# VectorE's maxima, reciprocals and scalings as jobs of their own, and Strassen's scheme in the first channel product from batch 5 on

## The chip, the cores and the metric

The kernel runs on one core of one Trainium2 chip. The metric is the time of one execution on the device, in microseconds (us); smaller is better. TensorE is called PE here (PEld is its weight load), VectorE DVE, ScalarE ACT, GpSimd POOL, and SyncE SP, as the profile calls them.

## What is computed

Two blocks in a row, on 8 batches of 576 rows. The first is linear attention with 8 heads of 64 columns and 128 random features, the second an MLP mixer over rows ("tokens") and columns ("channels"). Cut to what matters:

```python
def phi(x):                                   # x: q or k, scaled by 64 ** -0.25
    h = einsum('bhsd,md->bhsm', x, omega) - sum(x * x) / 2
    return exp(h - max(h)) / sqrt(m)
kv  = einsum('bhsm,bhsd->bhmd', phi(k), v);  z = sum(phi(k), over s)
x   = einsum('bhsm,bhmd->bhsd', phi(q), kv) / (einsum('bhsm,bhm->bhs', phi(q), z) + 1e-6)

h   = maximum(x.T @ w_tok1, 0) @ w_tok2       # over the 576 rows, 256 wide inside
u   = x + h.T
out = u + maximum(u @ w_ch1, 0) @ w_ch2       # 512 columns, 1536 wide inside
```

## The kernel before

Everything runs in fp16 with sums in fp32. Each batch has 512 main rows and 64 tail rows; the tail rows of all batches are gathered and go through the channel block together at the end, as a ninth "batch" (c == B in the code).

A batch passes through these stages. **Loads**: POOL's DMAs write q and k to scratch in DRAM as fp16, SP's transposing DMAs bring them back with heads along partitions (`load_transposed`), into rings `kT` and `qT` of three buffers; `v` has a ring of three too. **Attention** (`attention`): PE makes the features of k (`kp`) and q (`qp`) for a pair of heads, 64-row matmuls that run two side by side; ACT takes the exponential out of PSUM. DVE takes the largest feature of each row of `kp` (`reduce_max`, into `km`) and its reciprocal, which goes into the last column of `vs`; POOL scales `v` by it. PE makes `kv`, then for each head the numerators and the denominator (function `num`, five matmuls of 65 columns into one PSUM bank), and DVE takes the reciprocal of the denominators (`rc`) and multiplies (`num_out`), which gives `x`. **Token mixing** (`token_mix`): two products on PE, a ReLU between them, and DVE's additions that give `u`; one transposing DMA on SP makes `uT` of it. `token_tail` does the tail rows of a pair of batches. **Channel mixing** (`channel_mix`): the first product, u @ w_ch1, its ReLU into `r3`, and the second product.

Strassen's scheme does a product of 2 x 2 blocks with seven block products in place of eight, for extra sums. The second channel product uses it from batch 1 on (`channel_out_fast`). The first uses it for batches `c >= FAST1` (`channel_in_fast`), with `FAST1 = 6`; before that it is the plain product of line 1120, 48 matmuls of 512 columns whose 12 banks ACT (in some cases DVE) reads with a ReLU. In the fast form each of three passes makes seven products of four matmuls of 256 columns in three PSUM banks X, Y, Z; ACT or DVE copies X out between products (`kept`, `go_a`), DVE adds the copies (`summed`, line 1066), and some ReLUs are done in place afterwards. Four sums of `u` blocks (`go_u`) go ahead of it on DVE, and once in the kernel four sums of weight blocks (`first_weights`). The summed weights and the sums of u live in buffers taken from the rings: `HOME` and `OF_V` name one buffer each of kT, qT and v, and the copies take one of x and one of r1. From `FAST1` on each of these five rings has a buffer less.

No scheduler decides the order. The code lists jobs (`plan.add`, 1293 of them), each for one engine, with what it depends on. The table `ORDER` gives the order in which their instructions are written out, `SLOT` the buffer of a ring or the PSUM bank that each takes, and `MOVED` the engine of some jobs. Each engine then runs its own instructions strictly in that order. A job's function may issue several instructions, and nothing of the same engine comes between them.

Of the kernel before, what the change touches and what calls it, by code (L numbers as in the profile page):

```python
# [9 lines left out]
FP32 = mybir.dt.float32  # L10
# [57 lines left out]
]  # L68
SLOT = (
# [22 lines left out]
class Job:  # L92
    def __init__(self, eng, cost, key, fn, deps, take, give, rows, wire):
        self.eng, self.cost, self.key, self.fn = eng, cost, key, fn
        self.deps, self.take, self.give = deps, take, give
        self.rows, self.wire = rows, wire
        self.end = None
        self.heavy = False

FAST1 = 6


def covered(name):

    kind = name[0][0] if isinstance(name[0], tuple) else name[0]
    if kind in ("X", "Y", "Z"):
# [71 lines left out]
def kernel(  # L180
# [92 lines left out]
    t_kmt = ring(2, [P, 4], FP16, "kmt")  # L273
    kt_nb = sb([P, 2, 2], FP32, "kt_nb")
    t_rct = ring(2, [P, 4], FP16, "rct")
    t_rc = ring(4, [P, 2, NJ + 1], FP32, "rc")


    nat = {}
# [946 lines left out]
```

## Time and profile before

| | |
|---|---|
| time, median of 3 runs | 279.74 us (279.21 to 279.97) |
| the profiled execution, its own time | 279.72 us |
| its span, first to last instruction | 277.9 us |
| busy share of the span | PE 96%, DVE 84%, ACT 56%, POOL 33% |
| granted clock of PE, mean | 0.974 |
| DVE instructions | 487 |
| DMA | 39.69 MB, 143 GB/s on average |

The 1.8 us between the span and the execution's own time lie around the first and the last instruction. A busy PE includes the latency of each matmul, which overlaps the next one, so PE's real load is read from the distance between starts. A group's row gives the busy time, the mean duration of one instruction in ns, and the idle time of the engine just ahead of them.

### The profile page before, as it was taken

The page shows a single profiled execution, that of the slowest core. Times are in us where ns is not written, and L with a number is a line of the kernel's source. Part 1 is how long each engine was busy: PE and PEld are TensorE (multiplying, and loading weights), DVE is VectorE, ACT ScalarE, POOL GpSimd, SP SyncE. Part 2 cuts the span into 40 slices and gives each one's busy share as a digit, 9 for nine tenths or more (in the row PEclk, how much of TensorE's full clock was granted, in tenths as well). Part 3 has the DMA queues.
Part 4 walks back from the last instruction along what each step waited for, and adds up shares of the span by engine and source line. Part 5 has one row for each costly group of instructions (what it writes and reads, how often), then busy time and mean ns, then how long its engine had stood idle before and what let it go on. Part 6 is the DMA issues. An engine that isn't in the chain of part 4 may idle for free.

```text
span 277.9 us, 6547 instructions
## 1 busy us (share of the span) xinstructions
PE 265.6 (96%) x2624; PEld 179.5 (65%) x2624; DVE 233.7 (84%) x487; ACT 154.5 (56%) x318; POOL 91.6 (33%) x115
## 2 busy tenths in 40 slices
PE   5789999999999999999999999999999999999993
PEld 2657546443657755665677646764597688888882
DVE  1698828499999889996998799999997999889992
ACT  2797994049667427644567544878835425153410
POOL 8597794007510773048006910333400000000000
PEclk9559999999999999999999999999999999999999
DMA  7999999999997999995989993970060062030125
GB/s 160 200 205 169 182 185 204 164 151 211 182 226 164 164 211 162 170 196 89 189 181 211 203 195 85 167 179 4 18 174 0 2 150 97 0 153 0 65 105 136
DMA packets 80622, 39.69 MB, mean 143 GB/s; under 512 B 63984, under 2 KB 76144, under 8 KB 80400
## 3 DMA queue, kind: packets, MB, share of 16 engines
q0 software_dynamic: 31696, 17.61, 44.0%
q1 hardware_dynamic: 47696, 18.52, 30.5%
q10 hardware_dynamic: 1200, 3.15, 3.2%
q8 instruction: 20, 0.33, 0.5%
q14 instruction: 10, 0.08, 0.1%
HBM read 35.95 MB, written 16.52 MB: 189 GB/s over the span
## 4 chain that ended last, share of the span: by engine, by line
PE 88%; DVE 4%; DMA 3%; ACT 2%; issue 1%; ACTq 0%; DVEq 0%
PE bank L965 25%; PE bank L1120 22%; PE bank L1053 9%; PE bank L833 5%; PE bank L820 5%; PE bank L1155 4%; PE bank L711 3%; PE bank L699 3%; DMA wc<-in_k_dram 3%; PE bank L777 3%; PE bank L744 2%; DVE o L954 1%; PE bank L887 1%; DVE x L787 1%; PE bank L859 1%; ACT qp L557 1%
## 5 line engine op out<-in xcount | busy, mean ns | idle before, releaser
L301 ACT ACTIVATE r<-bank 128x512 f16<-128x512 f32 (+1 forms) x82 | 46.3, 604 | 43.5 <-PE bank L1120 25.6
L1120 PE MATMUL bank<-uT,wc 128*128 128x512 f16 x280 | 67.9, 379 | 0.0
L306 POOL TENSOR_TENSOR vs<-v,vs 128x512 f16<-128x512 f16 x32 | 34.3, 1072 | 79.5 <-DVE vs L725 49.8
L1120 PEld LDWEIGHTS <-wc 128*128 128x128 f16 x280 | 24.8, 98 | 25.7 <-issue 2.6
L965 PEld LDWEIGHTS <-r 128*128 128x128 f16 x384 | 36.7, 98 | 6.9 <-issue 1.3
L557 ACT ACTIVATE qp<-bank 128x512 f16<-128x512 f32 x64 | 36.6, 624 | 8.0 <-PE bank L711 5.2
L557 ACT ACTIVATE kp<-bank 128x512 f16<-128x512 f32 x64 | 36.5, 617 | 7.2 <-PE bank L699 7.0
L723 DVE TENSOR_REDUCE km<-kp 128x8 f16<-128x1024 f16 x32 | 38.5, 1205 | 0.6 <-ACT kp L557 0.4
L787 DVE TENSOR_TENSOR x<-bank,rc 128x320 f16<-128x320 f32 x62 | 30.5, 492 | 2.1
L965 PEld LDWEIGHTS <-S 128*128 128x128 f16 x288 | 28.2, 98 | 5.3 <-issue 0.6
L999 POOL DMA_DIRECT2D out_dram<-o x1 | 0.7, 665 | 73.4 <-issue 73.4
L965 PE MATMUL bank<-T,r 128*128 128x256 f16 x192 | 23.8, 273 | 0.0
L965 PE MATMUL bank<-wc,r 128*128 128x256 f16 x192 | 23.6, 273 | 0.0
L965 PE MATMUL bank<-T,S 128*128 128x256 f16 x192 | 23.6, 273 | 0.0
L303 DVE TENSOR_SCALAR r<-bank 128x512 f16<-128x512 f32 (+1 forms) x26 | 17.1, 663 | 7.5 <-PE bank L820 4.9
L954 DVE TENSOR_TENSOR o<-u,bank 128x512 f32<-128x512 f16 x28 | 19.0, 679 | 2.8 <-PE bank L965 2.6
L836 DVE TENSOR_TENSOR u<-x,bank 128x512 f16<-128x512 f16 x28 | 17.6, 680 | 0.5 <-ACT r L297 0.5
L777 PEld LDWEIGHTS <-qp 128*128 128x128 f16 x256 | 13.7, 100 | 6.2 <-issue 0.2
L954 DVE TENSOR_TENSOR o<-o,bank 128x512 f32<-128x512 f32 (+1 forms) x25 | 15.1, 612 | 2.7 <-PE bank L965 2.5
L1053 PEld LDWEIGHTS <-wc 128*128 128x128 f16 x144 | 13.8, 98 | 2.6 <-issue 0.6
L777 PE MATMUL bank<-kvsb,qp 128*128 128x65 f16 x256 | 15.0, 196 | 0.0
L711 PE MATMUL bank<-qT,omT 64*128 64x512 f16 x64 | 12.5, 410 | 1.7 <-ACT qT L297 1.7
(151 smaller groups left out, 470.5 us busy)
## 6 DMA issues: line engine op xcount, KB each, us to landing
out_dram<-o SPq DMA_DIRECT2D x10, 512.0 KB, 2.9
q<-in_q_dram POOLq DMA_DIRECT2D x6, 576.0 KB, 9.6
wc<-in_moe_w_ch_dram POOLq DMA_DIRECT2D x4, 768.0 KB, 10.8
k<-in_k_dram POOLq DMA_DIRECT2D x6, 512.0 KB, 7.8
v<-in_v_dram POOLq DMA_DIRECT2D x6, 512.0 KB, 10.0
out_dram<-o ACTq DMA_DIRECT2D x4, 512.0 KB, 2.7
r<-in_q_dram POOLq DMA_DIRECT2D x4, 288.0 KB, 7.1
v<-in_v_dram POOLq DMA_DIRECT2D x4, 256.0 KB, 9.5
```

The costliest lines, as they stand in the source:

```text
L301: nc.scalar.activation(out=out, in_=in_, func=AF.Relu)
L306: (nc.gpsimd if eng == "POOL" else nc.vector).tensor_tensor(**kw)
L557: nc.scalar.activation(out=out, in_=in_, func=AF.Exp, bias=0.0, scale=1.0)
L711: nc.tensor.matmul(ps[e], omT[half[e]], t[half[e], 2 * hp : 2 * hp + 2, 0:R], start=True, stop=True)
L723: nc.vector.reduce_max(out=mx, in_=kpv, axis=AX.X)
L777: nc.tensor.matmul(ps[:, k, j * 65 : (j + 1) * 65], st, s[:, i, 0 : D + 1], start=True, stop=True)
L787: nc.vector.tensor_tensor(out=t_x[place("x", b)][:, :, (2 * hp + hs[0]) * D : (2 * hp + hs[0] + n) * D].rearrange("p j (i d) -> p i j d", ...
L836: nc.vector.tensor_tensor(out=t_u[place("u", b)][:, j, :], in0=t_x[place("x", b)][:, j, :], in1=bank(n), op=ALU.add)
L954: nc.vector.tensor_tensor(out=o, in0=a, in1=ps, op=ALU.add)
L965: nc.tensor.matmul(ps[:, j * DH : (j + 1) * DH], a[:, cb, j * P : (j + 1) * P], w[:, cb, :], start=(bank_of(b, j0) not in held and j == j0 ...
L1053: nc.tensor.matmul(ps[:, 2 * P * t : 2 * P * t + 2 * P], a_[:, k, cb * P : (cb + 1) * P], m[:, :, k, :], start=(begin and t == 0 and k == ...
L1120: nc.tensor.matmul(ps, wc1[:, db, cb * P : (cb + 1) * P], moving(db), start=(db == 0), stop=(db == ND - 1))
```

## The change

Seven edits of structure, and new tables:

- The job that took the maximum of `kp` and its reciprocal becomes two jobs, with a ring `km` of four buffers for the maxima (two before, used in turn).
- The same for the tail rows of k: maximum, reciprocal and product with the mask become three jobs.
- The reciprocal and the scaling of a head's numerators become two jobs, with a ring `rc` of six buffers.
- The two additions of `token_tail` become two jobs, each of which gives its batch's `x` free.
- `FAST1` goes from 6 to 5: batch 5's first channel product takes the fast form too, and the ring buffers for it are taken a batch earlier.
- `ORDER`, `SLOT` and `MOVED` are written anew, for 1431 jobs. No other constant changes.

```diff
@@ ORDER, its second row: the same jobs, with later numbers
-49, 18, 46, 69, 71, 45, 77, 120, 51, 90, 50, 105, 122, 82, 52, 106, 17, 107, 19, 53, 121, 54, 83, 111, 92, 123, 91, 30, 108, 124, 126, 72, 112, 79,
+49, 18, 46, 69, 71, 45, 77, 127, 51, 93, 50, 110, 129, 82, 52, 111, 17, 112, 19, 83, 128, 53, 54, 84, 116, 95, 130, 94, 30, 113, 117, 131, 133, 72,
...
-FAST1 = 6
+FAST1 = 5
...
-             "kvsb": 3, "ktt": 2, "x": 3, "r1": 3, "u": 3, "uT": 3, "r3": 2, "S": 1, "V": 1, "s": 3, "o": 2, "bank": 8}
+             "kvsb": 3, "ktt": 2, "x": 3, "r1": 3, "u": 3, "uT": 3, "r3": 2, "S": 1, "V": 1, "s": 3, "o": 2, "km": 4, "rc": 6, "bank": 8}
...
-    t_km = ring(2, [P, 8], FP16, "km")
+    t_km = ring(COUNT["km"], [P, 8], FP16, "km")
...
-    t_rc = ring(4, [P, 2, NJ + 1], FP32, "rc")
+    t_rc = ring(COUNT["rc"], [P, NJ + 1], FP32, "rc")
...
-            j_ktm = add("DVE", 1.2, kkt + 0.01, kt_max, deps=[*j_kte, j_msk], take=[("vbd", b)] if dma_in else [])
+            j_ktm = add("DVE", 0.7, kkt + 0.01, kt_red, deps=[*j_kte, *kt_parts.get(b - 2, [])])
...
+            j_ktr = add("DVE", 0.2, kkt + 0.01, kt_rec, deps=[j_ktm])
...
+            j_ktm = add("DVE", 0.2, kkt + 0.01, kt_vb, deps=[j_ktr, j_msk], take=[("vbd", b)] if dma_in else [])
+            kt_parts[b] = [j_ktr, j_ktm]
...
             def km(hp=hp):
                 kpv = t_kp[place("kp", (b, hp))].rearrange("p c e m -> p (c e) m")
-                mx, vs = t_km[hp % 2], t_vs[place("vs", (b, hp))]
-                nc.vector.reduce_max(out=mx, in_=kpv, axis=AX.X)
+                nc.vector.reduce_max(out=t_km[place("km", (b, hp))], in_=kpv, axis=AX.X)
+            j_m = add("DVE", 1.2, at_["km"], km, deps=je, take=[("km", (b, hp))])
+            def km_rec(hp=hp):
                 with nc.allow_low_precision(reason="fp16 operand of the matmul"):
-                    nc.vector.reciprocal(out=vs[:, :, D], in_=mx)
-            j_m = add("DVE", 1.4, at_["km"], km, deps=je, take=[("vs", (b, hp))])
+                    nc.vector.reciprocal(out=t_vs[place("vs", (b, hp))][:, :, D], in_=t_km[place("km", (b, hp))])
+            j_m = add("DVE", 0.2, at_["km"], km_rec, deps=[j_m], take=[("vs", (b, hp))], give=[("km", (b, hp))])
...
+                def rec(where=where, rc_of=rc_of):
+                    nc.vector.reciprocal(out=rc_of(), in_=where()[:, 0, 0 : 5 * 65].rearrange("p (j d) -> p j d", d=65)[:, :, D])
+                kno = HEAD["no"][2 * hp + hs[0]] if b == 0 else at_["no"]
+                j_r = add("DVE", 0.22, kno - 0.3, rec, deps=[j_n], take=[n_rc])
...
-                    last_x.append(add("DVE", 0.1 + 0.52 * len(hs), kno, num_out, deps=[j_n], take=[("x", b)], give=[at]))
+                    last_x.append(add("DVE", 0.62, kno, num_out, deps=[j_r], take=[("x", b)], give=[at, n_rc]))
...
-        def uadd():
-            for o in range(2):
-                s = half[o]
+        j2 = []
+        for o in range(2):
+            def uadd(o=o, s=half[o]):
                 nc.vector.tensor_tensor(out=t_ut[s, pair_], in0=t_x[place("x", 2 * pair_ + o)][s, NJ, :], in1=bank(n)[s], op=ALU.add)
-        j2 = add("DVE", 1.36, key, uadd, deps=[j1], give=[("bank", n), ("x", 2 * pair_), ("x", 2 * pair_ + 1)])
+            j2.append(add("DVE", 0.69, key, uadd, deps=[j1], give=[("bank", n), ("x", 2 * pair_ + o)]))
```

The new tables show in the order of each engine's instructions. On PE it is the same up to the middle of batch 3's channel products, the 1006th matmul, and another after it.

The first place is DVE in batch 4's attention, where it scales the heads into the `x` buffer 119 (`rc` are the reciprocals, `bank` the PSUM banks with the numerators). Before:

```order
L786 RECIPROCAL rc_144<-bank_67 128x5
L787 TENSOR_TENSOR x_119<-bank_67,rc_144 128x5x64
L786 RECIPROCAL rc_143<-bank_63 128x5
L787 TENSOR_TENSOR x_119<-bank_63,rc_143 128x5x64
L786 RECIPROCAL rc_143<-bank_65 128x5
L787 TENSOR_TENSOR x_119<-bank_65,rc_143 128x5x64
```

The same place in the changed program, where lines 798 and 802 are the reciprocal and the scaling:

```order
L798 RECIPROCAL rc_144<-bank_65 128x5
L798 RECIPROCAL rc_148<-bank_70 128x5
L802 TENSOR_TENSOR x_119<-bank_70,rc_148 128x5x64
L798 RECIPROCAL rc_147<-bank_67 128x5
L798 RECIPROCAL rc_145<-bank_68 128x5
L802 TENSOR_TENSOR x_119<-bank_67,rc_147 128x5x64
L802 TENSOR_TENSOR x_119<-bank_65,rc_144 128x5x64
L802 TENSOR_TENSOR x_119<-bank_64,rc_143 128x5x64
```

A scaling no longer has to follow its own reciprocal; most now read one that was made two or more instructions earlier.

The second place is DVE where the last weight sum (`wc<-wc`) and the sums of u stand for the first batch that takes the fast form. Before, that is batch 6 (`uT_127`), amid batch 7's attention:

```order
L306 TENSOR_TENSOR wc_80<-wc_80 128x2x768
L306 TENSOR_TENSOR S<-r_131 128x768
L306 TENSOR_TENSOR r_131<-r_131 128x3x256 x2
L306 TENSOR_TENSOR S<-S,r_131 128x768 x2
L954 TENSOR_TENSOR o_133<-u_125,bank_66 128x2x256
L786 RECIPROCAL rc_144<-bank_68 128x5
L787 TENSOR_TENSOR x_119<-bank_68,rc_144 128x5x64
L954 TENSOR_TENSOR o_132<-o_132,bank_70 128x2x256
L786 RECIPROCAL rc_144<-bank_69 128x5
L787 TENSOR_TENSOR x_119<-bank_69,rc_144 128x5x64
L306 TENSOR_TENSOR kT_89<-uT_127 128x512
```

In the changed program it is batch 5 (`uT_129`), amid batch 6's attention, which begins to write `x_119` only after both additions of the tail rows (`ut`):

```order
L904 TENSOR_TENSOR ut<-x_119,bank_70 64x512
L904 TENSOR_TENSOR ut<-x_120,bank_70 64x512
L312 TENSOR_TENSOR wc_80<-wc_80 128x2x768
L965 TENSOR_TENSOR o_132<-o_132,bank_65 128x2x256
L312 TENSOR_TENSOR kT_88<-uT_129 128x512
L312 TENSOR_TENSOR qT_85<-uT_129,kT_88 128x512
L965 TENSOR_TENSOR o_133<-u_124,bank_63 128x2x256
L303 CAST kvsb_117<-bank_67 128x2x65
L312 TENSOR_TENSOR uT_129<-uT_129 128x2x256
L312 TENSOR_TENSOR v_92<-uT_129,qT_85 128x512
L798 RECIPROCAL rc_146<-bank_69 128x5
L802 TENSOR_TENSOR x_119<-bank_69,rc_146 128x5x64
```

The preparation has moved a batch earlier, and the buffers that it uses are now kT_88 and qT_85, not kT_89 and qT_86.

The third place is SP's queue around batch 7's transposing loads. Before:

```order
L841 DMA_TRANSPOSE uT_129<-u_125 128x16x128
L391 DMA_TRANSPOSE kT_88<-k_7_158 128x1x2304
L1006 DMA out_dram<-o_133 128x1024
L898 DMA_TRANSPOSE uTt<-ut 128x4x128
L391 DMA_TRANSPOSE qT_85<-q_7_157 128x1x2304
L841 DMA_TRANSPOSE uT_127<-u_126 128x16x128
```

In the changed program (line 397 is the load, 852 the transpose of u, 909 that of the tail rows, 1017 a store):

```order
L852 DMA_TRANSPOSE uT_129<-u_125 128x16x128
L397 DMA_TRANSPOSE kT_89<-k_7_162 128x1x2304
L909 DMA_TRANSPOSE uTt<-ut 128x4x128
L397 DMA_TRANSPOSE qT_86<-q_7_161 128x1x2304
L1017 DMA out_dram<-o_132 128x1024
L852 DMA_TRANSPOSE uT_127<-u_126 128x16x128
```

Batch 7's k and q go into the buffers of batch 5 (89 and 86), where they went into those of batch 4 before; a store now stands between them and the transpose of batch 6's u.

More of the change, by code (lines that the diff above doesn't have):

```diff
@@ L23 @@
 3, 0, 4, -1, 14, 7, 5, 2, -2, 6, 10, 1, -3, -4, 9, -5, 8, -6, -7, 12, -8, 11, 13, 41, 21, 38, 42, 47, 22, 39, 43, 40, 48, 67, 76, 68, 44, 78, 16, 70,
[44 rows of a table removed]
[50 rows of a table added]
 ]
 SLOT = (
-    "00010203010320452601510723430621530411262070250331643571201036502170160175130200671135462167340123201201243172160135071304056117337611405242"
-    "13273212406745307413212050264111070260542300073561240011137632413005114726002203221170220145370200325123340671206511070032241107321540103201"
-    "03221711413101305210117250024012410731211721602132040570040260230570105337110602202613531013270127021523120021003514126240340212031451203032"
-    "41501013607204010631112714023363060140123010700341200603001222417502456140325317630401502630207412036051222306433131263411051015001251652212"
-    "17420335106022716422067513013651427021650113122704252064750022201364170051213500121641000756420657142526126202141024061102150670314510226130"
-    "7150014306102710200210171032071505"
+    "00010203010320452601510723430620153041112620702502331643357120103650201170213601754130502067113541260167342103201002124317016013507112043256"
+    "11733711640035413223730462501750432752130563212000415161270410052300273011450021611713451320032657211022406324147303245250672013023063044536"
+    "35217120104172006325142763105042322106324711501134026002211147302035022413512376011104024526132071054200103760124002413532002715430073006511"
+    "01225316124030412023107151034520743222354154042740201503671410140761153203301600256113211110026523710201230135205167323114001010723430602554"
+    "11670121327324115002534406501273200310650742013356022223124037051143202615170161422302034612146312500046100343313114015210056231102643100605"
+    "23071431112020302542170003514113203043120720370722250504712073310250170251136050214103105002671421060040126205700265110002410063507106"
@@ L76 @@
 )
 MOVED = {
-43: "ACT", 51: "ACT", 54: "ACT", 60: "ACT", 63: "ACT", 65: "ACT", 75: "DVE", 85: "ACT", 129: "ACT", 139: "DVE", 141: "DVE", 145: "ACT", 147: "DVE",
-163: "ACT", 169: "DVE", 171: "ACT", 175: "DVE", 179: "ACT", 190: "ACT", 194: "ACT", 228: "ACT", 242: "DVE", 256: "DVE", 265: "DVE", 278: "DVE", 280:
-"DVE", 286: "DVE", 300: "DVE", 324: "ACT", 399: "DVE", 426: "DVE", 428: "DVE", 432: "DVE", 434: "DVE", 484: "DVE", 498: "DVE", 552: "DVE", 556: "DVE",
-562: "DVE", 593: "ACT", 594: "ACT", 634: "DVE", 662: "DVE", 690: "DVE", 692: "DVE", 700: "DVE", 702: "DVE", 768: "DVE", 796: "DVE", 864: "ACT", 972:
@@ L82 @@
-"DVE", 988: "DVE", 1003: "ACT", 1105: "DVE", 1125: "DVE", 1127: "DVE", 1134: "DVE", 1157: "DVE", 1165: "ACT", 1203: "DVE", 1233: "DVE", 1242: "ACT",
-1244: "ACT", 1282: "SP", 1283: "SP", 1285: "ACT", 1286: "SP", 1287: "ACT", 1288: "SP", 1289: "ACT", 1290: "SP", 1291: "ACT", 1292: "SP",
+43: "ACT", 51: "ACT", 54: "ACT", 60: "ACT", 63: "ACT", 65: "ACT", 75: "DVE", 86: "ACT", 137: "ACT", 149: "DVE", 151: "DVE", 155: "ACT", 157: "DVE",
+173: "ACT", 179: "DVE", 181: "ACT", 185: "DVE", 189: "ACT", 200: "ACT", 204: "ACT", 244: "ACT", 261: "DVE", 278: "DVE", 289: "DVE", 303: "DVE", 305:
@@ new lines @@
+"DVE", 311: "DVE", 325: "DVE", 349: "ACT", 438: "DVE", 457: "DVE", 465: "DVE", 473: "DVE", 497: "ACT", 543: "DVE", 588: "DVE", 610: "DVE", 614: "DVE",
+728: "DVE", 760: "DVE", 772: "DVE", 796: "ACT", 825: "DVE", 876: "DVE", 935: "DVE", 950: "ACT", 951: "ACT", 952: "ACT", 977: "ACT", 1023: "DVE", 1040:
+"DVE", 1057: "DVE", 1086: "DVE", 1114: "DVE", 1125: "ACT", 1126: "ACT", 1197: "DVE", 1267: "DVE", 1279: "DVE", 1286: "DVE", 1288: "DVE", 1293: "DVE",
+1302: "ACT", 1379: "ACT", 1382: "ACT", 1419: "ACT", 1421: "SP", 1427: "ACT", 1428: "SP",
@@ L562, in vbd_of @@
         return first_vbd[:, b] if b < NPE else t_vbd[place("vbd", b)]
+    kt_parts = {}
     def attention(b, key, step):
@@ L629, in attention, with kt_red, kt_rec, kt_vb @@
                 j_kte.append(add("ACT", 0.3, kkt, kt_exp, deps=[j_kt], take=[("kpt", b)], give=[("bank", (n_kt, e))]))
-            def kt_max():
-                kp = t_kpt[place("kpt", b)].rearrange("p g e m -> p (g e) m")
-                mx, rc, vb = t_kmt[b % 2], t_rct[b % 2], vbd_of(b)
-                nc.vector.reduce_max(out=mx, in_=kp, axis=AX.X)
+            def kt_red():
+                nc.vector.reduce_max(out=t_kmt[b % 2], in_=t_kpt[place("kpt", b)].rearrange("p g e m -> p (g e) m"), axis=AX.X)
+            j_ktm = add("DVE", 0.7, kkt + 0.01, kt_red, deps=[*j_kte, *kt_parts.get(b - 2, [])])
+            def kt_rec():
                 with nc.allow_low_precision(reason="fp16 operand of the matmul"):
-                    nc.vector.reciprocal(out=rc, in_=mx)
+                    nc.vector.reciprocal(out=t_rct[b % 2], in_=t_kmt[b % 2])
+            j_ktr = add("DVE", 0.2, kkt + 0.01, kt_rec, deps=[j_ktm])
+            def kt_vb():
                 nc.vector.tensor_tensor(
-                    out=vb[:, :, 0:nh, D],
-                    in0=rc.unsqueeze(2).broadcast_to((P, 4, nh)),
+                    out=vbd_of(b)[:, :, 0:nh, D],
+                    in0=t_rct[b % 2].unsqueeze(2).broadcast_to((P, 4, nh)),
                     in1=msk.unsqueeze(1).broadcast_to((P, 4, nh)),
@@ L781, in attention, with rc_of @@
                           give=[("qp", (b, hp)), ("kvsb", (b, hp)), ("qpt", b)])
-                def num_out(hp=hp, hs=hs, where=where):
-                    n = len(hs)
-                    ps = where()[:, :, 0 : 5 * 65].rearrange("p i (j d) -> p i j d", d=65)
-                    rc = t_rc[2 + hp % 2][:, hs[0] : hs[0] + n]
-                    nc.vector.reciprocal(out=rc, in_=ps[:, :, :, D])
+                n_rc = ("rc", (b, hp, hs[0]))
+                def rc_of(n_rc=n_rc):
+                    return t_rc[place(*n_rc)]
@@ L787, in num_out @@
+                def rec(where=where, rc_of=rc_of):
+                    nc.vector.reciprocal(out=rc_of(), in_=where()[:, 0, 0 : 5 * 65].rearrange("p (j d) -> p j d", d=65)[:, :, D])
+                kno = HEAD["no"][2 * hp + hs[0]] if b == 0 else at_["no"]
+                j_r = add("DVE", 0.22, kno - 0.3, rec, deps=[j_n], take=[n_rc])
+                def num_out(hp=hp, i=hs[0], where=where, rc_of=rc_of):
                     nc.vector.tensor_tensor(
-                        out=t_x[place("x", b)][:, :, (2 * hp + hs[0]) * D : (2 * hp + hs[0] + n) * D].rearrange("p j (i d) -> p i j d", i=n),
@@ L789, in num_out @@
-                        in0=ps[:, :, :, 0:D],
-                        in1=rc.unsqueeze(3).broadcast_to((P, n, NJ + 1, D)),
+                        out=t_x[place("x", b)][:, :, (2 * hp + i) * D : (2 * hp + i + 1) * D],
+                        in0=where()[:, 0, 0 : 5 * 65].rearrange("p (j d) -> p j d", d=65)[:, :, 0:D],
+                        in1=rc_of().unsqueeze(2).broadcast_to((P, NJ + 1, D)),
                         op=ALU.mult,
                     )
-                kno = HEAD["no"][2 * hp + hs[0]] if b == 0 else at_["no"]
@@ L794, in attention, with scale @@
                 if b == 0 and BY["no"][2 * hp + hs[0]] == "A":
-                    def rec(hp=hp, i=hs[0], where=where):
-                        nc.vector.reciprocal(out=t_rc[hp % 2][:, i], in_=where()[:, 0, 0 : 5 * 65].rearrange("p (j d) -> p j d", d=65)[:, :, D])
-                    def scale(hp=hp, i=hs[0], where=where):
+                    def scale(hp=hp, i=hs[0], where=where, rc_of=rc_of):
                         for j in range(NJ + 1):
                             nc.scalar.activation(out=t_x[place("x", b)][:, j, (2 * hp + i) * D : (2 * hp + i + 1) * D],
-                                                 in_=where()[:, 0, j * 65 : j * 65 + D], func=AF.Copy, scale=t_rc[hp % 2][:, i, j : j + 1])
@@ L801, in attention @@
-                    j_r = add("DVE", 0.22, kno - 0.3, rec, deps=[j_n])
-                    last_x.append(add("ACT", 1.1, kno, scale, deps=[j_r], take=[("x", b)], give=[at]))
+                                                 in_=where()[:, 0, j * 65 : j * 65 + D], func=AF.Copy, scale=rc_of()[:, j : j + 1])
+                    last_x.append(add("ACT", 1.1, kno, scale, deps=[j_r], take=[("x", b)], give=[at, n_rc]))
                 else:
-                    last_x.append(add("DVE", 0.1 + 0.52 * len(hs), kno, num_out, deps=[j_n], take=[("x", b)], give=[at]))
+                    last_x.append(add("DVE", 0.62, kno, num_out, deps=[j_r], take=[("x", b)], give=[at, n_rc]))
@@ L1187 @@
         channel_mix(b, float(b), uT)
-    tails = [tail_transpose(i, 7.1 + 0.1 * i, [j, ld["kT", B - 1]]) for i, j in enumerate(tails)]
+    tails = [tail_transpose(i, 7.1 + 0.1 * i, [*j, ld["kT", B - 1]]) for i, j in enumerate(tails)]
     channel_mix(B, float(B), tails)
```

92 rows, old and new, of the table ORDER are left out of this document.

## The prediction

> **What bounds the kernel now.** The profiled execution took 279.72 us, 0.02 under the median of the runs shown (279.74), so sums against it need no correction. I read first the page's busy shares, then the chain of work that ended last, then what PE waited for, then the busy time by stage.
>
> ```profile
> PE 265.6 (96%) x2624; PEld 179.5 (65%) x2624; DVE 233.7 (84%) x487; ACT 154.5 (56%) x318; POOL 91.6 (33%) x115
> 161.48 4.32 PE bank L1120 x20
> 231.57 3.50 PE bank L1053 x32
> 264.34 9.21 PE bank L965 x84
> 273.57 0.42 DVE o L954
> ```
>
> The first line is the page's; the others are four pieces of the chain (start, length, what). The chain is PE nearly everywhere: a plain first product runs at 4.32 / 20 = 0.216 us for 512 columns, a fast one at 3.50 / 32 = 0.1094 us for 256, and the last 84 matmuls run without a hole until DVE's last addition. So PE's busy share is no artefact of its latency. PE's waits in the part that the change reorders, from 79.8 us (the first token product of batch 2) to the end, were these:
>
> ```profile
> PE bank L965 <- DVE o L954: 0.5, 1, 0.5
> PE bank L699 <- DVE x L787: 0.2, 1, 0.2
> PE bank L1053 <- ACT bank L297: 0.2, 1, 0.2
> ```
>
> 0.9 us in all (us in total, times, longest). The rest is stages, each from one batch's first token product to the next one's:
>
> ```profile
> core 0: us, PE busy (x) PEld busy (x) DVE busy (x) ACT busy (x) POOL busy (x), PEclk, DMA share, GB/s
> 79.83:108.31 28.48, 28.48 (x275) 18.33 (x273) 25.72 (x54) 15.28 (x32) 13.02 (x16) 1.00 1.02 183
> 108.31:137.49 29.18, 29.18 (x291) 18.63 (x289) 25.69 (x55) 16.24 (x33) 9.58 (x11) 1.00 0.99 163
> 137.49:166.49 29.00, 29.00 (x281) 18.46 (x279) 26.24 (x56) 17.76 (x37) 12.15 (x14) 1.00 1.14 198
> 166.49:191.59 25.10, 24.83 (x266) 16.21 (x263) 24.02 (x49) 18.37 (x38) 4.86 (x5) 1.00 0.59 120
> 191.59:214.45 22.86, 22.70 (x225) 16.12 (x224) 21.41 (x47) 14.27 (x30) 5.28 (x5) 1.00 0.24 60
> 214.45:273.60 59.15, 58.63 (x518) 50.14 (x515) 52.58 (x104) 21.18 (x37) 0.67 (x1) 1.00 0.22 73
> ```
>
> PE fills each stage at full clock; DVE comes next, at 88 to 96%. So PE's work sets the time, and DVE is what can spoil it: most where batches 5 to 7 overlap (24.02 of 25.10 us).
>
> **The change part by part.** *PE's work.* The program loses 48 matmuls of 512 columns and gains 84 of 256: 48 x 0.216 = 10.37 against 84 x 0.1094 = 9.19, so -1.18 us. All its other matmuls are the same in number and shape. This is on the path in full, since PE is.
>
> *PE's changes of shape.* Going between full matmuls and side-by-side half ones costs a little.
>
> ```profile
> 171.26 1.47 PE L965 MATMUL bank<-T,S 128*128 128x256 f16 x12
> 172.67 0.62 PE L887 MATMUL bank<-r,w 128*64 128x512 f16 x4
> 173.22 0.39 PE L711 MATMUL bank<-qT,omT 64*128 64x512 f16 x2
> ```
>
> Twelve matmuls from 171.26 at 0.1094 should end at 172.57, and the next start is 0.10 later; L887's two pairs of 512 columns should end at 173.10, and L711 starts 0.12 later. Past the point where the orders part, the old order goes into half matmuls 18 times, the new one 20 times (+2 in, +2 out), and changes among half shapes 23 against 19 times (-4). At 0.1 us each that is +0.4 - 0.4 = 0.
>
> *DVE's work.* Batch 5's fast product brings six additions out of PSUM (L1066) and four sums of u blocks; two copies of kvsb come to DVE by the new table; four ReLUs out of PSUM go, and one output addition, which ACT's copy of a bank replaces.
>
> ```profile
> L1066 DVE TENSOR_TENSOR r<-x,bank 128x512 f16<-128x512 f32 x12 | 8.2, 681 | 0.0
> L306 DVE TENSOR_TENSOR kT<-uT 128x512 f16<-128x512 f16 x2 | 0.8, 417 | 0.0
> L297 DVE CAST kvsb<-bank 128x130 f16<-128x130 f32 x10 | 2.9, 291 | 7.4 <-PE bank L753 5.1 <-PE bank L751 2.2
> L303 DVE TENSOR_SCALAR r<-bank 128x512 f16<-128x512 f32 x24 | 16.2, 683 | 6.7 <-PE bank L820 4.9 <-PE bank L1053 1.0 <-PE bank L1120 0.8
> L954 DVE TENSOR_TENSOR o<-o,bank 128x512 f32<-128x512 f32 x19 | 12.7, 674 | 2.3 <-PE bank L965 2.0
> L297 ACT COPY x<-bank 128x512 f32<-128x512 f32 x11 | 6.4, 587 | 13.3 <-PE bank L1053 7.2 <-DVE r L1066 6.1
> L301 ACT ACTIVATE r<-r 128x1024 f16<-128x1024 f16 x2 | 2.1, 1069 | 1.3 <-DVE r L1066 1.3
> ```
>
> 6 x 0.681 + 4 x 0.417 + 2 x 0.291 - 4 x 0.683 - 0.674 = +2.9 us on DVE. ACT gets ten copies of 0.587 and four ReLUs in place of at most 1.069, under 10.2 us on an engine that is busy 154.5 of 277.9: hidden, unless one of its copies between two products of a bank comes late (0.2 us for such a wait above).
>
> *DVE's joints.* What the split is worth shows where a reciprocal and its scaling follow each other.
>
> ```profile
> 163.85 0.18 DVE L786 RECIPROCAL rc<-bank 128x5 f32<-128x5 f32 x1
> 164.07 0.49 DVE L787 TENSOR_TENSOR x<-bank,rc 128x320 f16<-128x320 f32 x1
> 164.47 0.18 DVE L786 RECIPROCAL rc<-bank 128x5 f32<-128x5 f32 x1
> ```
>
> The scaling, which reads the reciprocal, starts 0.04 us after its end (163.85 + 0.18 against 164.07); the next reciprocal, which needs nothing of the scaling, starts 0.09 us ahead of its end (164.07 + 0.49 against 164.47). So an instruction that reads what the one just ahead of it wrote costs some 0.12 us more than a free one. In the reordered part the old order has 62 such joints out of the split jobs, the new one 18; elsewhere six come to be. 38 x 0.12 = 4.6 us less. DVE needs 2.9 - 4.6 = -1.7 us: despite Strassen it gets a little freer.
>
> The Trainium skill speaks against this term: in "VectorE: DVE Perf Modes", section "The DRAIN you can't avoid", the next Vector instruction does not start until the pipeline is empty, and its "Rules for kernel authors" say to minimise the count of instructions, not their semaphores. By that rule the joints would be worth nothing and DVE's sum would be +2.9. The three rows above disagree: the free instruction starts ahead of the end.
>
> *Buffers and queues.* Batch 7's k and q wait for batch 5's features in place of batch 4's, but stand on SP behind the transpose of batch 5's u, as before; the features are done well ahead of that, so nothing waits there: 0. On SP a store now stands ahead of batch 6's uT, for which PE's first product waits. The store needs DVE's last addition of batch 4, which stands just ahead of the additions that uT itself needs: 0. The uT chain is what may show:
>
> ```profile
> 169.54 1.89 PE L833 MATMUL bank<-r,w 128*128 128x512 f16 x8
> 170.64 2.47 DVE L836 TENSOR_TENSOR u<-x,bank 128x512 f16<-128x512 f16 x4
> 173.18 1.89 SPq L841 DMA_TRANSPOSE uT<-u  x1
> uT<-u SPq DMA_TRANSPOSE x7, 5.0
> ```
>
> From the end of the second token product (169.54 + 8 x 0.216 = 171.27) to the landing (173.18 + 5.0) are 6.9 us. In the new order batch 6 has 6.4 us of matmuls between them, and some 0.6 us of changes of shape: the cover is just enough. If DVE is late with the four additions, PE waits; bounds 0 and about 1 us, and I take 0. The last store after the last matmul is of the same kind as before: 0.
>
> **Sum.** 279.72 - 1.18 + 0 (shapes) + 0 (waits: 0.9 before, and as many after) = 278.54, say 278.5.
>
> **The rivals.** A measurement of this kernel can tell about 0.3% (0.84 us) from no change, so faster means under 278.9 and slower over 280.6.
>
> *The waits go as well.* DVE has 1.7 us less to do, and two of the three waits above ended on DVE. Then 278.5 - 0.9 = 277.6; with four half shapes' changes less than I count (0.4), 277.2. Against it: waits of a few tenths come from the order, which is another one. Chance 0.12.
>
> *Part of it is given back.* Batch 6's uT lands 0.7 us late, or ACT's copies hold up three or four products by 0.2 us each: 278.5 + 0.7 = 279.2, no change that can be told. For it: the cover above is bare, and the chain of product, copy, product of the fast form is longer than that of a plain product and a ReLU. Chance 0.18.
>
> *DVE becomes the bound over batches 6 and 7.* Between the first token products of these two the new order has 27.2 us of matmuls and 61 DVE instructions, 32.2 us at the groups' means; 56 of them are free and take 0.085 us back, which leaves 27.7. Going on for 31 us of matmuls from there, DVE's need exceeds PE's by 2.8 us. If DVE enters this stretch without a lead, PE waits for all of it: 278.5 + 2.8 = 281.3. It decides once DVE trails PE by more than the buffers allow, two or three banks. Against it: in the old order's stage from 166.49 us, by the same count, DVE needed 26.0 us for 23.4 us of matmuls, and PE's waits there were one of 0.2 us. For it: this stretch is longer, and the x ring has one buffer less already in it. Chance 0.15.
>
> *The joints give nothing*, as the page's rule would have it, and DVE, 2.9 us fuller, is the bound: 278.5 + 2.9 = 281.4. The rows of 164 us speak against it. Chance 0.03. That the change does not part the pairs at all is ruled out by the order, for the part after 102 us; ahead of it nothing moves.
>
> **How the numbers follow.** My forecast has the remaining 0.52, of which some 0.04 lies over 278.9. Faster: 0.12 + 0.48 = 0.60. No change: 0.18 + 0.04 = 0.22. Slower: 0.18. The range goes from the first rival's end, 277.2, to the third's, 281.3; beyond these lie under 2 in 10.
>
> **What would show it.** Right: the first products of batch 5 as 84 matmuls at 0.109 us; starts on PE without holes; DVE busy a little less over the reordered part; rows where a reciprocal starts ahead of the end of what stands before it. The waits of PE from 79.8 us on should stay near 0.9 us. Wrong: waits of PE for DVE's `x` or `o` between batch 6's and batch 7's token products that add up to over 1.5 us; a wait for `uT` at batch 6's first product; or PE's work falling by something other than 1.2 us.

## The result, and the profile after

The changed kernel takes 281.68 us (median of 4 runs, 281.45 to 281.86) against 279.78 us: ratio 1.0071, 95% interval 1.0053 to 1.0088. It is slower by 1.9 us, 0.4 us beyond the upper end of the range. A second set of runs gave 281.55 us and 1.0073 (1.0059 to 1.0087).

The page's busy line, then PE's waits from 80.6 us (batch 2's first token product) to the end, then the stages from one first token product to the next, with the columns of before:

```profile
PE 266.9 (95%) x2660; PEld 182.7 (65%) x2660; DVE 235.7 (84%) x494; ACT 161.3 (58%) x328; POOL 92.5 (33%) x115
```

```profile
PE bank L789 <- DVE kvsb L303: 0.7, 1, 0.7
PE bank L976 <- DVE o L965: 0.4, 1, 0.4
PE bank L1064 <- DMA uT<-u: 0.4, 1, 0.4
```

```profile
80.64:109.86 29.22, 29.22 (x287) 18.60 (x288) 25.80 (x54) 18.25 (x38) 13.02 (x16) 1.00 1.02 191
109.86:138.49 28.63, 28.51 (x273) 18.30 (x272) 25.34 (x55) 14.27 (x30) 9.62 (x11) 1.00 1.14 180
138.49:169.00 30.51, 29.70 (x292) 18.86 (x292) 28.06 (x54) 19.56 (x41) 12.20 (x13) 1.00 0.98 182
169.00:196.87 27.87, 27.43 (x297) 21.01 (x296) 26.21 (x57) 18.75 (x36) 5.28 (x5) 1.00 0.55 91
196.87:225.85 28.98, 28.62 (x307) 22.23 (x306) 27.68 (x63) 20.88 (x41) 5.86 (x6) 1.00 0.32 66
225.85:275.46 49.61, 49.57 (x433) 41.81 (x430) 43.74 (x88) 18.07 (x32) 0.67 (x1) 1.00 0.24 76
```

PE is as busy as before, but it now waits 0.81 us in the stage from 138.49 us (30.51 less 29.70), where it waited for nothing. And batch 2's first token product starts at 80.6 us in place of 79.8, although all that PE does up to there is the same. The same stretch in one row, from the first matmul of that product to the last of the kernel, before:

```profile
79.83:273.15 193.32, 192.44 (x1840) 137.80 (x1839) 175.44 (x359) 103.09 (x204) 45.55 (x52) 1.00 0.64 126
```

After:

```profile
80.57:275.04 194.47, 192.74 (x1877) 140.80 (x1876) 176.72 (x366) 109.79 (x214) 46.64 (x52) 1.00 0.66 126
```

So 0.74 us are lost ahead of the reordered part (80.57 less 79.83) and 1.15 us in it (194.47 less 193.32), together the 1.9 us of the measurement.

What stands behind both is seen when DVE's rows are read beside POOL's. Four places of the changed kernel (start, length, what; in each fence DVE's rows, then POOL's):

```profile
18.61 1.37 DVE L684 COPY qpt<-qpt 128x512 f16<-128x512 f16 x1 [0.20 <-ACT qpt L563]
...
18.76 1.07 POOL L312 TENSOR_TENSOR vs<-v,vs 128x512 f16<-128x512 f16 x1
```

```profile
121.15 1.83 DVE L312 TENSOR_TENSOR S<-r,S 128x768 f16<-128x768 f16 x2
...
121.38 1.19 POOL L312 TENSOR_TENSOR vs<-v,vs 128x512 f16<-128x512 f16 x1 [1.54 <-DVE vs L737]
```

```profile
154.57 1.75 DVE L312 TENSOR_TENSOR kT<-wc 128x1536 f16<-128x1536 f16 x1
156.36 1.70 DVE L312 TENSOR_TENSOR qT<-kT,wc 128x1536 f16<-128x1536 f16 x1
...
155.79 3.17 POOL L312 TENSOR_TENSOR vs<-v,vs 128x512 f16<-128x512 f16 x2
```

```profile
171.25 1.46 DVE L312 TENSOR_TENSOR S<-r,S 128x768 f16<-128x768 f16 x1
...
171.24 1.05 POOL L312 TENSOR_TENSOR vs<-v,vs 128x512 f16<-128x512 f16 x1 [9.67 <-DVE S L312]
```

The copy took 0.29 us before the change (at 18.80 us), the sums S take 0.55 us and the weight sums 0.95 us elsewhere. Beside a scaling of v on POOL they take 0.75 to 1.08 us more: five instructions, 4.4 us of DVE in all. The DVE instructions that read PSUM don't care (in three traces, of before, after and the four waits below, the additions that give `u` take 0.67 to 0.69 us, 76 of them free and 8 beside POOL), nor do the maxima (a median of 1.21 us for 43 free ones and for 53 beside POOL). Where PE stands still follows in the chain that ended last:

```profile
158.76 1.09 DVE km L733
160.03 0.56 DVE kmt L639
...
172.64 0.54 DVE S L312
173.27 0.58 DVE o L965
...
202.67 6.14 DMA uT<-u
```

A stall is counted below as the distance between the starts of two matmuls less the pitch of the first, which is a little more than the waits show. By the starts of the same matmuls in both traces PE is 0.55 us late at 22 us, behind the copy, and 0.97 us at 33 us, of which 0.74 are left at 80 us. In the reordered part it stalls behind DVE 0.29 us at 126.3, 0.88 and 0.25 us at 160, and 0.58 us at 173.1: 2.0 us. Batch 6's uT adds 0.53 us at 208.2. The old order's four stalls past 102 us (some 1.6 us) are gone, but four smaller ones are new, at 185, 187, 228 and 246.6 us (0.74 us in all).

### The profile page after: what moved, and what is told of

It is laid out like the page before. It is cut to its first block, busy times and chain, and to the rows that moved or that the text cites. A ratio compares the mean times of both kernels' runs of the same rounds, so it can differ in the third digit from the quotient of the medians.

```text
span 279.9 us, 6635 instructions
## 1 busy us (share of the span) xinstructions
PE 266.9 (95%) x2660; PEld 182.7 (65%) x2660; DVE 235.7 (84%) x494; ACT 161.3 (58%) x328; POOL 92.5 (33%) x115
## 4 chain that ended last, share of the span: by engine, by line
PE 79%; DVE 9%; ACT 4%; DMA 4%; issue 2%; DVEq 0%
PE bank L976 22%; PE bank L1131 17%; PE bank L1064 13%; PE bank L831 5%; PE bank L1166 4%; PE bank L844 3%; PE bank L710 3%; PE bank L789 2%; PE bank L722 2%; DMA uT<-u 2%; PE bank L756 2%; DMA wc<-in_k_dram 2%; DVE u L847 2%; DVE km L733 1%; ACT kp L563 1%
## 5 line engine op out<-in xcount | busy, mean ns | idle before, releaser
L307 ACT ACTIVATE r<-bank 128x512 f16<-128x512 f32 (+1 forms) x80 | 45.2, 601 | 33.5 <-PE bank L1131 18.5
L312 POOL TENSOR_TENSOR vs<-v,vs 128x512 f16<-128x512 f16 x32 | 35.3, 1108 | 81.5 <-DVE vs L737 38.3
L1131 PE MATMUL bank<-uT,wc 128*128 128x512 f16 x232 | 55.8, 379 | 0.1
L802 DVE TENSOR_TENSOR x<-bank,rc 128x320 f16<-128x320 f32 x62 | 29.0, 485 | 1.2
L309 DVE TENSOR_SCALAR r<-bank 128x512 f16<-128x512 f32 (+1 forms) x22 | 14.4, 658 | 7.7 <-PE bank L831 3.6
L312 POOL TENSOR_TENSOR vbd<-vt,vbd 128x512 f16<-128x512 f16 x6 | 6.3, 1058 | 33.6 <-DVE vbd L646 20.5
```

The source lines that it names most:

```text
L307: nc.scalar.activation(out=out, in_=in_, func=AF.Relu)
L309: nc.vector.tensor_relu(out=out, in_=in_)
L312: (nc.gpsimd if eng == "POOL" else nc.vector).tensor_tensor(**kw)
L802: nc.vector.tensor_tensor(out=t_x[place("x", b)][:, :, (2 * hp + i) * D : (2 * hp + i + 1) * D], in0=where()[:, 0, 0 : 5 * 65].rearrange(" ...
L1131: nc.tensor.matmul(ps, wc1[:, db, cb * P : (cb + 1) * P], moving(db), start=(db == 0), stop=(db == ND - 1))
```

## The experiments

Theory P: DVE's copies and sums that read only SBUF and POOL's scalings hold each other up, and PE pays where DVE has no lead. Rival O: the new order costs PE the same in any case, and a removed stall comes back in another place. All ratios are against the kernel before, run on the same chip beside the kernel in question. Differences between two changed kernels are taken from medians of different chips; by the ratios they come out up to 0.3 us otherwise.

**Four waits.** One edit tells the two apart with no work taken away: POOL's scaling waits until the DVE instruction beside it is done. The planner's loop gets a table of POOL's jobs and the DVE jobs that they wait for:

```diff
+AFTER = {101: 75, 726: 477, 874: 901, 1004: 776}
...
             j.fn()
+            if n in AFTER.values():
+                last[n] = traced[-1].name
+            if n in AFTER:
+                tc.add_manual_dep(traced[n0], last[AFTER[n]], sync, reason="port")
```

The first pair is the early copy, the others are the three late places. Early alone:

> The changed kernel (281.68 us) with one wait added: POOL's fourth scaling of v in batch 0 waits for DVE's copy qpt<-qpt, which in the changed kernel took 1.37 us beside that scaling (0.29 us before the change). Nothing is left out. Theory P (DVE's copies and sums that read and write only SBUF stand still while POOL's product runs, and PE pays for that): the copy takes 0.3 us again, PE is 0.8 us earlier at 34 us and to the end, 280.9 us. Rival O (the new order costs PE the same in other places): no change at the end, 281.5 to 281.9 us.

Measured 280.73 us, ratio 1.0034 (1.0017 to 1.0051); the copy takes 0.29 us again. Late alone:

> The changed kernel with three waits added: POOL's scalings of v at 121.4, 155.8 and 171.2 us wait for the DVE sums that took 1.41, 1.75 and 1.70, and 1.46 us beside them. Nothing is left out. Theory P: these sums take 0.55 and 0.95 us again, and PE's stalls behind them (0.29 at 126.3, 0.88 and 0.25 at 160, 0.58 at 173.1 us) go: 281.7 - 2.0 = 279.7 us. Rival O: the stalls come back on other buffers, 281.3 us or more. Rival W (POOL's scalings come late by the wait and hold up PE's kv): slower than 281.7 us.

Measured 279.90 us, ratio 1.0016 (1.0000 to 1.0033). The stalls at 160 and 173.1 us go (1.71 us). The one at 126.3 us does not: in this kernel and in the next PE still stalls 0.26 us there, although the sum S ahead of it takes 0.55 us again. So the collision at 121 us costs DVE time, but PE nothing that shows. All four:

> The changed kernel with all four waits. Theory P: 281.7 - 0.8 - 2.0 = 278.9 us, about what the prediction gave without any new stall. Rival O: 281 us or more.

Measured 278.77 us, ratio 0.9972 (0.9960 to 0.9985): faster than the kernel before. Against the control's 281.55 us (below) the early wait gives 0.8 us, the late ones 1.65, and all four 2.8. Its rows at the weight sums, and the stretch of above in one row:

```profile
153.50 0.95 DVE L323 TENSOR_TENSOR kT<-wc 128x1536 f16<-128x1536 f16 x1
154.49 0.96 DVE L323 TENSOR_TENSOR qT<-kT,wc 128x1536 f16<-128x1536 f16 x1
...
155.59 2.06 POOL L323 TENSOR_TENSOR vs<-v,vs 128x512 f16<-128x512 f16 x2 [0.88 <-DVE qT L323]
```

```profile
79.61:271.98 192.37, 192.18 (x1876) 140.66 (x1875) 173.98 (x366) 109.77 (x214) 45.39 (x52) 1.00 0.66 126
```

Both sums are back at 0.95 us. POOL, although it waits 0.88 us, ends its two scalings 4.15 us after the first sum's start (155.59 + 2.06 - 153.50), where it took 4.39 us without the wait (155.79 + 3.17 - 154.57): W is out. So is O: by the starts no stall is new, PE is idle 0.19 us in the whole stretch (192.37 less 192.18), and the stretch is 2.1 us shorter than after, 0.95 shorter than before.

**The control**, the changed kernel once more:

> The changed kernel itself once more, as the control beside the others of this call: 281.7 us, with the same DVE rows of 1.37, 1.41, 1.75, 1.70 and 1.46 us beside POOL's scalings if the collisions come from the order, and other ones if they come by chance in each execution.

281.55 us, and the same five DVE rows (1.37, 1.41, 1.76, 1.70, 1.30 us): the collisions belong to the order.

**Four buffers for the maxima in the kernel before**, for the early loss:

```diff
-    t_km = ring(2, [P, 8], FP16, "km")
+    t_km = ring(4, [P, 8], FP16, "km")
...
-                mx, vs = t_km[hp % 2], t_vs[place("vs", (b, hp))]
+                mx, vs = t_km[hp % 4], t_vs[place("vs", (b, hp))]
```

> The kernel before the change (279.78 us), with four buffers for the maxima in place of two and nothing else. If the early loss of 0.8 us comes from the ring of maxima (DVE no longer waits for a buffer, so the copy qpt<-qpt starts at another moment against POOL's scaling), this kernel loses it too: the copy takes 1.4 us and the time is 280.6 us. If it comes from another part of the change (the split jobs, the order), the time stays at 279.8 us.

280.52 us, ratio 1.0028 (1.0015 to 1.0041): slower by 0.8 us by the ratio, 0.95 by the medians. (In its profiled execution PE is some 0.45 us late already at 9.5 us, ahead of the first maximum, so the loss is read from the runs.) The rows of the kernel before, then of this one:

```profile
18.80 0.29 DVE L673 COPY qpt<-qpt 128x512 f16<-128x512 f16 x1
...
18.94 1.07 POOL L306 TENSOR_TENSOR vs<-v,vs 128x512 f16<-128x512 f16 x1
```

```profile
19.26 1.37 DVE L673 COPY qpt<-qpt 128x512 f16<-128x512 f16 x1 [0.20 <-ACT qpt L557]
...
19.40 1.07 POOL L306 TENSOR_TENSOR vs<-v,vs 128x512 f16<-128x512 f16 x1
```

In the kernel before, the maximum ahead of the copy starts 0.11 us after the end of the reciprocal before it (17.39 against 17.07 + 0.21 us), with four buffers 0.09 us ahead of that end (17.65 against 17.53 + 0.21). So the bigger ring alone makes DVE reach the copy 0.2 us earlier, and it has to wait for ACT. In both kernels the copy then starts 0.03 us after ACT is done and 0.14 us ahead of the scaling by the records; in one it gets through and in the other it is held. That DVE stood idle just ahead of it is the one difference seen in the rows; why this decides it stays open.

**Both kernels' older collisions.** Batch 2 has the same thing in both kernels, at the sums T for the second product; before the change:

```profile
63.91 0.91 DVE L490 TENSOR_TENSOR T<-wc,T 128x1536 f16<-128x1536 f16 x1
64.73 1.81 DVE L490 TENSOR_TENSOR T<-wc 128x1536 f16<-128x1536 f16 x1
...
64.24 1.49 POOL L306 TENSOR_TENSOR vs<-v,vs 128x512 f16<-128x512 f16 x1
```

The sum that starts 0.33 us ahead of the scaling goes free, and the scaling takes 1.49 us in place of 1.05; the next sum is held in its turn. Two more waits, with POOL's two scalings written out behind the sums (`BEHIND = {427: 36, 410: 37}`, and the same pairs in `AFTER`), in the kernel of the four waits and, as 390 and 376, in the kernel before:

> The changed kernel with the four waits (278.77 us) and two more, at 64 and 70 us, where both kernels have the same collision: POOL's scalings of v in batch 2 are written out behind the sums T<-wc and wait for them. Nothing is left out. Theory P: the two sums take 0.95 us in place of 1.81, and PE's stall of 0.71 us at 66.4 us goes: 278.1 us. If DVE's slack behind 70 us or a late POOL takes it back: 278.6 to 279 us.

278.46 us, ratio 0.9972 (0.9954 to 0.9989): 0.3 us less than with four waits by the medians, the same by the ratios, so no gain is shown.

> The kernel before the change with the same two waits of POOL for T<-wc, and nothing else. Theory P holds without the change too: 279.6 - 0.7 = 278.9 us. If the stall at 66.6 us has another cause: 279.6 us.

278.98 us, ratio 0.9988 (0.9977 to 1.0000): 0.6 us less by the medians, 0.3 by the ratio, whose interval reaches 1. The stall of 0.71 us is gone in both, but POOL, put behind the second sum, is late for `kv` at 71 us, by 0.49 and 0.30 us; this is the first kernel's only wait of PE from 60 us on:

```profile
PE bank L783 <- POOL vs L339: 0.3, 1, 0.3
```

**The joints.** In the kernel of the four waits every reciprocal of denominators goes right ahead of its own scaling on DVE again, which makes 66 such neighbours of 40. (That most scalings of the changed kernel no longer directly follow their own reciprocal holds past 102 us, where 12 of 38 still do by the trace; in the whole kernel 36 of 62 do.)

```diff
+            order.remove(n)                  # n: rec, m: its num_out
+            order.insert(order.index(m), n)
```

> The changed kernel with the four waits, and every reciprocal of denominators put back right ahead of its scaling on DVE: 66 of 71 reciprocals are followed by their own scaling, 40 without this edit. Nothing is left out. If a joint costs 0.12 us, DVE needs 26 x 0.12 = 3.1 us more; its rows show starts 0.04 us after the end. If DVE has no slack in batches 4 to 7, PE pays most of it, 280 to 281.9 us; if it has, the time stays within 0.3 us of 278.8. If joints cost nothing, DVE's sum of busy time and short gaps doesn't grow.

279.66 us, ratio 1.0003 (0.9990 to 1.0015), 0.9 us more than with the pairs apart. The same stretch in this kernel:

```profile
81.40:274.89 193.49, 192.76 (x1876) 140.93 (x1875) 176.57 (x366) 110.03 (x214) 45.47 (x52) 1.00 0.67 126
```

DVE's busy time grows from 173.98 to 176.57 us, 2.6 us for 26 joints, 0.10 each, and the stretch by 1.12 us. (Its profiled execution lost 1.8 us ahead of 80 us and is long by that, so only the stretch is compared.) A joint has its price, and less than half of it reaches the end.

**Less work on PE.** In the kernel of the four waits 21 of the 84 matmuls of one batch's fast first product are left out, in batch 5 and, in another kernel, in batch 7:

```diff
-                        for k in range(2):
+                        for k in range(1 if c == 5 and t else 2):
```

> The changed kernel with the four waits, and 21 of the 84 matmuls of batch 5's fast first product left out (the second row block of each product's second half). If PE's work is on the path in full there: 278.8 - 21 x 0.1094 = 276.5 us. If DVE or ACT, with the copies and additions of the fast form, sets the time between batch 5's and batch 6's first products: less than half of the 2.3 us, 277.7 us or more.

> The changed kernel with the four waits, and 21 of the 84 matmuls of batch 7's fast first product left out, as in batch 5's before, which took only 0.55 us off. In this stretch DVE has no attention work left. If PE alone sets the time there: 278.8 - 2.3 = 276.5 us. If the fast form's own chain of copies and additions is what held batch 5's: 278 us or more here too.

278.22 us (0.9955, 0.9941 to 0.9969) and 278.18 us (0.9949, 0.9936 to 0.9962): 2.3 us of PE's work less bring 0.5 to 0.6 us in either place. In batch 5 PE now waits for DVE's sums of u and scalings:

```profile
183.12 0.50 PE L1075 MATMUL bank<-qT 128*128 128x256 f16 x3 [0.30 <-DVE qT L323]
...
185.22 0.28 PE L800 MATMUL bank<-kvsb,qp 128*128 128x65 f16 x4 [0.28 <-DVE x L813]
```

In batch 7, with no attention left, its waits are for copies of banks and sums of u, the fast form's own chain:

```profile
PE bank L1075 <- DVE x L314: 0.6, 1, 0.6
...
PE bank L1075 <- DVE qT L323: 0.2, 1, 0.2
```

**A better version.** With a fifth wait for the first sum T<-wc alone, and two sums S of batch 5 behind the additions that batch 6's uT needs (`BEHIND = {427: 36, 956: 1070, 957: 956}`):

> The changed kernel with the four waits, a fifth for the first sum T<-wc at 64 us (POOL's scaling of batch 2 behind it), and two sums S of batch 5 put behind the four additions that batch 6's uT waits for. Nothing is left out. By theory P: 278.77 - 0.71 (the stall at 66.4 us; POOL is free until 68.5 us, so its delay should not show this time) - 0.23 (the stall at 205.5 us) = 277.8 us. If the stalls only change their place: 278.5 us or more.

279.31 us, ratio 0.9998 (0.9984 to 1.0013): the stall at 66 us is gone, but the second product needs the sums S before uT:

```profile
201.61 1.16 PE L1003 MATMUL bank<-T,S 128*128 128x256 f16 x9 [0.60 <-DVE S L339]
```

Without that second edit:

> The changed kernel with the four waits and the one for the first sum T<-wc at 64 us alone; the second at 70 us and the order of the sums S stay as they are in the changed kernel, since there the first edit brought a late POOL (0.49 us at 70.8 us) and the second a late S (0.77 us at 200.7 us). Nothing is left out. By theory P: 278.77 - 0.71 = 278.1 us. If a new stall takes it back: 278.5 us or more.

278.64 us (278.40 to 282.48 in 6 runs), ratio 0.9980 (0.9942 to 1.0017). The sum T<-wc takes 0.95 us, but in its profiled execution PE, now earlier, waits for a load of k:

```profile
PE bank L737 <- DMA kT<-k: 0.4, 1, 0.4
```

Its median is 1.2 us under that of the kernel before, its interval too wide to rank it. The kernels with four and six waits are the ones shown faster than both the kernel before and the changed one.

## Why the prediction was wrong, point by point

- **The step that failed** is "waits: 0.9 before, and as many after". It priced DVE's work by the means of groups and took these as free of what POOL does at that moment. The new order lays four of DVE's long sums beside POOL's scalings; they cost DVE 3.3 us and PE 1.7 us, by the stalls that go with the late waits (1.71) and by the runs (1.65). PE's waits in the reordered part, which the sum took as unchanged at 0.9 us, went from 0.88 to 1.73 us (193.32 less 192.44, and 194.47 less 192.74), beside stalls too short to show as waits, and that part is 1.15 us longer than before, where the sum has it 1.18 us shorter. The profile of before had a sign of it that I passed over: of two sums T<-wc of one shape one took 1.81 us and the other 0.95, behind a group mean of 1.38, and PE stalled 0.71 us behind the slow one.
- **"Ahead of it nothing moves"** was wrong. PE's program is the same there, DVE's timing isn't: four buffers for the maxima take a wait of DVE away, and 0.8 us are lost at the copy. The kernel before with nothing but that ring loses the same.
- **PE's work**, -1.18 us: right in size. At the pitches of 0.1093 and 0.2158 us the whole matmuls of the stretch need 1.18 us less; PE's busy time falls by 0.26 only (192.44 to 192.18), since it also holds the changes of shape and stalls shorter than a matmul's latency. With the collisions taken out the kernel is 0.80 us faster by the runs (0.95 us over the stretch). But "on the path in full, since PE is" holds only for about as much as was taken: the next 2.3 us brought 0.5 to 0.6, so DVE follows PE closely.
- **PE's changes of shape**, 0: wrong rule, small error. By the starts, a visit to half matmuls (from full ones to side-by-side half ones and back) costs 0.20 us in all, and changes among half shapes of 64 rows inside it nothing. The kernel before:

```profile
199.53 0.22 PE L751 MATMUL bank<-vbd,kpt 128*128 128x130 f16 x1
199.68 0.61 PE L711 MATMUL bank<-qT,omT 64*128 64x512 f16 x4
200.22 1.05 PE L965 MATMUL bank<-wc,r 128*128 128x256 f16 x8
```

  The 130 columns should end at 199.53 + 0.057 = 199.59, the next start is 0.09 later; the two pairs end at 199.68 + 2 x 0.216 = 200.11, the next is 0.11 later. With 20 visits for 18 that is +0.4 us, where the text subtracted 0.4 for changes inside.
- **DVE's sum**, 2.9 - 4.6 = -1.7 us: right once the collisions are out. DVE's busy time over the stretch goes from 175.44 to 173.98 us, -1.5. The joint is 0.10 us against 0.12 forecast. The rival that joints give nothing is ruled out.
- **Batch 6's uT**: the rival's mechanism came, 0.53 us late for its 0.7 (landing after 6.1 us, where the median before was 5.0), beside the main cause. It is 0.39 us in the control and 0.23 with the four waits. Of the three signs of being wrong that the text names, this wait alone came; DVE's waits came one and two batches earlier than it looked.
- **DVE as the bound over batches 6 and 7** gave the right size (281.3) by luck: between those batches' first token products PE waits 0.4 us in all, for the uT (28.98 less 28.62). Its working is also a little off: 32.2 - 56 x 0.085 is 27.4 us, or 27.6 with 0.04 for each of the other five, not 27.7, and how 2.8 us come of it over the next 31 us isn't worked out.

The Trainium skill states the rule that I left out, in "SBUF — State Buffer", section "Who interferes with whom": a DVE instruction with two SBUF inputs contends with a GpSimd instruction that reads SBUF, one with at most one SBUF input outside the two-port modes does not, and who issues first has the shared ports for the whole instruction. On which forms are hit, all rows here agree (sums of two SBUF inputs and the plain copy, 0.75 to 1.08 us longer; additions out of PSUM and maxima, nothing); the copy, with its one SBUF input, fits only if it ran in a two-port mode, which no run here shows. On who goes first the records agree in part: sums that start 0.2 us or more ahead of the scaling went free, all but the first weight sum, and scalings beside such sums took up to 1.49 us in place of 1.05. Closer than that they don't decide: a copy that starts 0.14 us ahead went free once and was held once.

## What to carry to other kernels

Read DVE's rows beside POOL's: an instruction that takes about twice its group's shortest beside a POOL product points to a collision, and a group's mean hides it. When a table of orders is written anew, or a ring only made bigger, ask which sums out of SBUF now fall beside POOL's work; a wait on the engine with slack (POOL is busy 33%) buys the busy one its full speed, as long as POOL's result doesn't come late by it (0.3 to 0.5 us at 71 us here). Work taken off the busiest engine is worth its time only up to the lead of the next one: here 2.3 us more of it brought 0.5 to 0.6.

## What the runs showed of the hardware

- A DVE sum and a POOL scaling run one behind the other, not both slower: at 171.2 us POOL's takes its usual 1.05 us and the sum, 0.55 us long when free, ends 0.42 us after it; at 156 us DVE's sum holds POOL's second scaling in turn (3.17 us for two, 2.06 in the kernel of the four waits).
- The first weight sum at 154.57 us took 0.80 us more, though POOL's records overlap it by 0.53 us only, at its end. The wait on POOL's scaling cures it, so that scaling is the cause; POOL's DMA issues beside the sum (from 154.63 us) are there with the wait too (from 153.57 us) and cost it nothing. Why it is held so early stays open.
- A visit to half matmuls costs 0.20 us whatever is in it (14 of the 18 visits past 102 us in the kernel before, by the starts; two others hold a stall, and two a change between halves of rows and halves of columns, which costs 0.12 us more).
